# GpSimd's long operations in four pieces, and the first low weight part made by VectorE

## The chip, the cores and the metric

The kernel runs on one core of a Trainium2 chip. A core has five engines that the program feeds with one queue each: TensorE (PE: matrix products and transpositions), VectorE (DVE), ScalarE (ACT), GpSimd (POOL) and SyncE (SP, which here issues most DMA transfers). Engines wait for each other by semaphores. The metric is the time of one execution in device microseconds; the time before is the median of three runs.

## What is computed

The inputs are float32: q, k, v of 4 batches x 8 heads x 576 tokens x 64, and the weights of three stages. Cut to what matters:

```python
# 1. causal attention and a linear memory, mixed by a gate per head
a = softmax(mask(q @ k.T / 8));  local = a @ v
phi = where(x > 0, x, exp(x) - 1) + 1
mem = (phi(q) @ M_prev) / (phi(q) @ z_prev + 1e-6)
x = sigmoid(beta) * mem + (1 - sigmoid(beta)) * local     # -> 2304 x 512
# 2. a mixture of 8 experts: each token goes to the expert of its largest logit
e = argmax(x @ w_gate);  y = gate_w * sigmoid(x @ w_output_gate)[e] * (relu(x @ w1[e]) @ w2[e])
# 3. a gated layer
out = (sigmoid(y @ m2_gate) * (y @ m2_val)) @ m2_out
```

## The kernel before

The three stages follow one another: attention with the routing to 320 or 340 us, the experts to about 659, the gated layer to the end. Precision is kept by splitting operands into a high and a low part (x rounded by ScalarE, then x minus that by VectorE or GpSimd).

The attention works on 16 pairs of heads, two pairs to a group `gi` (8 groups). For a pair TensorE transposes q and k, forms the scores of both heads in the two halves of its array (`scores`, L373), VectorE subtracts the mask and takes the row extremes (`masked`, L402), ScalarE exponentiates (L410), TensorE transposes the result (L455), either VectorE or ScalarE copies it (`copy`, L301 and L299), and TensorE multiplies it with v (L489). The reciprocals of the row sums are made by `recip`: a `scalar_tensor_tensor` (L420), a reciprocal (L421), a cast (L422) and a subtraction (L423), all of VectorE and 9 columns wide, from tiles in SBUF.

Beside this, for each group, phi(q) is made: ScalarE's `phi_exp` (L269), then four operations of GpSimd in `phi_sum` (n = 0 to 3: a maximum with 0, L274, a minimum with 1, L276, their sum, L278, the product with z, L280), VectorE's `phi_norm` (the sum `nm` of 64 columns each, L285 to L288) and GpSimd's `phi_scale` (L292). All of GpSimd's are 128 x 1152 (18 blocks of 64).

When the eight heads of a batch are finished, `Routing` computes logits, the largest logit and its place (`first`, L864 to L869: O), the gate's factors in four steps (`factor_a` L885 to L889 and a sum L875 or L878; `factor_b`, ScalarE's two exponentials L893 and L894; `factor_c` L901 to L903; `factor_d` L907), and x is stored to DRAM (`x_turn`, `x_keep`, `x_store`). With the last batch `slots` counts the tokens of each expert (L946, L953 and on to L1030: A), `row_sel` makes Bm (L997), a product of both (L1047) gives the tokens' places, and GpSimd gathers the first two tiles of tokens (L1063).

The first expert's weights, eight parts of 128 x 1024, are split at the end of the attention: the high parts `wh` by ScalarE (L1154), the low parts `wl` by VectorE or GpSimd (L1159).

The order of all this is made by `Plan`, which takes each step with a rank, a cost per engine and what it needs, and writes the instructions in the order of a greedy list; a step that names two engines goes to the one that the plan has free first. What an operation really takes, or that one engine holds up another, is not in the plan.

Of the kernel before, what the change touches and what calls it, by code (L numbers as in the profile page):

```python
# [9 lines left out]
F32 = mybir.dt.float32  # L10
# [3 lines left out]
ALU = mybir.AluOpType  # L14
# [4 lines left out]
P = 128  # L19
B, H, S, D = 4, 8, 576, 64  # L20
HG = 4
NP = B * H // 2
NQ = 9
NK = 5
# [5 lines left out]
NT = NTOK // P  # L30
# [25 lines left out]
class Plan:  # L56
# [15 lines left out]
    def add(self, name, rank, cost, fn, needs=(), takes=(), uses=()):  # L72

        assert name not in self.steps, name
        self.steps[name] = (rank, cost, fn, tuple(needs), tuple(takes))
        for t in (*takes, *uses):
            self.users.setdefault(t, []).append(name)
# [48 lines left out]
class Attention:  # L126
# [142 lines left out]
        self.nc.scalar.activation(self.G[gi, "e"], self.G[gi, "q"], AF.Exp)  # L269

    def phi_sum(self, gi, n):
        nc, q, ph, e = self.nc, self.G[gi, "q"], self.G[gi, "ph"], self.G[gi, "e"]
        if n == 0:
            nc.gpsimd.tensor_scalar(ph, q, 0.0, None, ALU.max)  # L274
        elif n == 1:
            nc.gpsimd.tensor_scalar(e, e, 1.0, None, ALU.min)  # L276
        elif n == 2:
            nc.gpsimd.tensor_tensor(ph, ph, e, ALU.add)  # L278
        else:
            nc.gpsimd.tensor_tensor(e, ph, self.G[gi, "z"], ALU.mult)  # L280

    def phi_norm(self, gi):
        nc = self.nc
# [5 lines left out]

    def phi_scale(self, gi):  # L290
        pv = self.G[gi, "ph"].rearrange("p (a d) -> p a d", d=64)
        self.nc.gpsimd.tensor_tensor(pv, pv, self.G[gi, "nm"][:, :, None].to_broadcast([P, 18, 64]), ALU.mult)  # L292


    GROUPS = ((0, 1, 2), (3, 4))
# [212 lines left out]
    def run(self, ex, change):  # L508
# [8 lines left out]
        add = p.add  # L517
# [10 lines left out]
        for gi in range(NP * 2 // HG):  # L528
            u0 = gi * NQ * (HG // 2)
            r = u0 - 18  # L530
            for l in range(2):
                for i, nm in enumerate("qk"):
                    add(("L", nm, gi, l), r + 2 * l + i, {"SP": 1.6}, lambda e, a=(gi, nm, l): self.load_nat(*a),
                        needs=[("L", nm, gi, 0)] * l, takes=[] if l else [(nm + "n", gi)], uses=[(nm + "n", gi)] * l)
# [7 lines left out]
            for n, c in enumerate((3.06, 3.06, 2.57, 2.57)):  # L542
                needs = [("L", "q", gi, 1)] if n == 0 else [("phe", gi)] if n == 1 else [("phs", gi, n - 1), ("phs", gi, 0)]
# [7 lines left out]
        for pi in range(NP):  # L551
            gi, u0 = pi // 2, pi * NQ
            before = [("S", pi - 2, c) for c in ORDER] if pi > 1 else []
            for g in range(2):
                n = (384, 192)[g]
                r = u0 - 13 + g
                for nm in "qk":
                    kz = nm == "k" and g == 0
                    add(("X", nm, pi, g), r, {"PE": PO + n / 1200}, lambda e, a=(nm, pi, g): self.turn(*a),
                        needs=[("L", nm, gi, pi % 2)] + (before if nm == "q" else [("X", "k", pi, 0)] if g else []),  # L560
# [3 lines left out]
                    needs=[("X", "q", pi, g)] + [("qh", pi, 0)] * g, takes=[] if g else [("qT", pi)], uses=[("T", ("q", pi, g))] + [("qT", pi)] * g)  # L564
                add(("ql", pi, g), r, {"DV": dv(nq)}, lambda e, a=(pi, g, 1): self.q_part(*a),
                    needs=[("qh", pi, g)], uses=[("T", ("q", pi, g)), ("qT", pi)])
                if g:
# [3 lines left out]
                    needs=[("X", "k", pi, g)] + ([("kh", pi, 0)] if g else []), uses=[("T", ("k", pi, g)), ("kz", pi)])  # L571
# [4 lines left out]
                    needs=[("ph", gi)] + ([("X", "ph", pi, 0)] if g else []),  # L576
                    takes=[("T", ("ph", pi, g))] + ([] if g else [("phT", pi)]), uses=[("ph", gi)])
                add(("pp", pi, g), r, {"AC": ac(n), "DV": dv(n)}, lambda e, a=(pi, g): self.p_part(e, *a),
                    needs=[("X", "ph", pi, g)] + ([("pp", pi, 0)] if g else []),
# [81 lines left out]
        wide = [n for n in p.steps if n[0] in ("phn", "qh", "ql", "zh", "zl", "S", "m", "r", "rt", "rk", "b", "bc", "t", "v", "o", "os")]  # L661
        for n in range(8):
            add(("wh", n), 900 + n, {"AC": 0.95}, lambda e: ex.split_hi(),
                needs=[("w", 7), ("lc", B - 1, 1), *wide] + ([("wh", n - 1)] if n else []) + [("xc", NT - 1 if n else NT - 4)])
            late = [] if n < 1 else [("r4", B - 1)] if n < 2 else ["places"] if n < 5 else ["x1"]
            add(("wl", n), 900 + n, {"DV": 1.14} if n in (2, 3, 4, 5) else {"PL": 2.3},
                lambda e, n=n: ex.split_lo(n, self.nc.vector if e == "DV" else self.nc.gpsimd), needs=[("wh", n)] + late)
        for n in range(2):
            add(("f", n), 998, {"SP": 1.0}, lambda e: ex.load_part(), needs=[("wl", n)] + ([("f", n - 1)] if n else []))
        add("ahead", 999, {"SP": 3.0}, lambda e: ex.load_ahead(self.gather), needs=["x1"] + [("wl", n) for n in range(4)])  # L670
# [398 lines left out]
class Experts:  # L1069
# [84 lines left out]
        self.nc.scalar.activation(hi, t, AF.Copy)  # L1154
        self.half[n] = t, hi, lo, slot

    def split_lo(self, n, eng):
        t, hi, lo, slot = self.half.pop(n)
        eng.tensor_tensor(lo, t, hi.bitcast(F32), ALU.subtract)  # L1159
        if slot is not None:  # L1160
            self.free.append(slot)

# [579 lines left out]
```

## Time and profile before

| | |
|---|---|
| median of three runs | 1142.98 us (1142.48 to 1143.62) |
| the profiled execution | 1142.84 us, its span 1140.9 us |
| TensorE busy over the span | 1039.0 us (91%) |
| VectorE busy | 547.2 us (48%) |
| ScalarE busy | 457.2 us (40%) |
| GpSimd busy | 275.0 us (24%) |
| mean granted TensorE clock | 0.952 |

The profile is of one execution. "Busy" counts from an instruction's start to its end; an instruction that is held by something other than a semaphore counts as busy while it is held. "Granted clock" is the share of TensorE's full clock in a stretch: 1.00 is 2.4 GHz, 0.50 is 1.2 GHz. In the timeline an idle time in brackets stands before an instruction and names what ended it.

### The profile page before, as it was taken

The page shows a single profiled execution, that of the slowest core. Times are in us where ns is not written, and L with a number is a line of the kernel's source. Part 1 is how long each engine was busy: PE and PEld are TensorE (multiplying, and loading weights), DVE is VectorE, ACT ScalarE, POOL GpSimd, SP SyncE. Part 2 cuts the span into 40 slices and gives each one's busy share as a digit, 9 for nine tenths or more (in the row PEclk, how much of TensorE's full clock was granted, in tenths as well). Part 3 has the DMA queues.
Part 4 walks back from the last instruction along what each step waited for, and adds up shares of the span by engine and source line. Part 5 has one row for each costly group of instructions (what it writes and reads, how often), then busy time and mean ns, then how long its engine had stood idle before and what let it go on. Part 6 is the DMA issues. An engine that isn't in the chain of part 4 may idle for free. (4 is left out here: it accounts for less than half of the span.)

```text
span 1140.9 us, 16928 instructions
## 1 busy us (share of the span) xinstructions
PE 1039.0 (91%) x6181; PEld 886.2 (78%) x6181; DVE 547.2 (48%) x1266; ACT 457.2 (40%) x1049; POOL 275.0 (24%) x268
## 2 busy tenths in 40 slices
PE   6799798899959969988996969999999999999997
PEld 4566566566648959977995758999899999999996
DVE  6878778777566244225323869961212112121112
ACT  5676576566445244125313445531221212221211
POOL 8464443142057135016303500000110000100101
PEclk9799899889979989998998979999999999999999
DMA  6847324223049348116513556510010000100000
GB/s 121 137 88 169 94 66 104 50 60 98 1 141 322 114 128 274 38 46 217 168 39 98 167 160 195 184 55 1 29 56 1 28 28 1 56 1 1 28 1 28
DMA packets 111900, 102.52 MB, mean 90 GB/s; under 512 B 69520, under 2 KB 86928, under 8 KB 111760
## 3 DMA queue, kind: packets, MB, share of 16 engines
q1 hardware_dynamic: 107888, 88.18, 27.3%
q0 software_dynamic: 3872, 12.62, 3.4%
q8 instruction: 70, 1.15, 0.5%
q14 instruction: 70, 0.57, 0.2%
HBM read 84.49 MB, written 16.28 MB: 88 GB/s over the span
## 5 line engine op out<-in xcount | busy, mean ns | idle before, releaser
L1539 DVE TENSOR_TENSOR G<-G,pT 128x384 f32<-128x384 f32 (+1 forms) x74 | 40.1, 543 | 248.9 <-PE pT L1525 247.4
L1571 POOL DMA_INDIRECT out_dram<-o,rows x18 | 17.5, 971 | 463.8 <-ACT o L1567 213.2
L1546 ACT ACTIVATE Gh<-G 128x384 fp32r<-128x384 f32 (+1 forms) x74 | 38.2, 516 | 162.1 <-DVE G L1539 162.1
L410 ACT ACTIVATE Sm<-Sm,mx 128x512 f32<-128x512 f32 (+3 forms) x144 | 83.2, 579 | 31.0 <-DVE mx L402 30.6
L1535 ACT ACTIVATE G<-pH 128x384 f32<-128x384 f32 x72 | 35.4, 491 | 128.1 <-PE pH L1525 128.0
L1159 POOL TENSOR_TENSOR W<-raw,W 128x1024 fp32r<-128x1024 f32 x23 | 61.4, 2668 | 102.4 <-ACT W L1154 102.3
L402 DVE CUSTOM_DVE_ANT_0 Sm<-Sp,mask 128x512 f32<-128x512 f32 (+3 forms) x144 | 65.1, 482 | 25.1 <-PE T L455 13.1
L455 PE MATMUL T<-ident,Sm 128*128 128x128 f32 (+1 forms) x400 | 66.1, 304 | 11.1 <-DVE xt L301 6.0
L1556 PE MATMUL pX<-W,Gh 128*128 128x512 f32 x220 | 68.8, 394 | 0.0
L1154 ACT ACTIVATE W<-raw 128x1024 fp32r<-128x1024 f32 x60 | 61.7, 1054 | 16.7 <-DMA y_dram<-y 7.9
L455 PEld LDWEIGHTS T<-ident,Sm 128*128 128x128 f32 (+1 forms) x400 | 47.7, 151 | 24.1 <-DVE xt L301 6.2
L299 ACT ACTIVATE pt<-T 128x512 f32<-128x512 f32 (+4 forms) x128 | 49.9, 434 | 32.3 <-PE T L455 31.2
L489 PE MATMUL O<-pt,vn 128*64 128x192 f32 (+4 forms) x512 | 60.6, 357 | 0.0
L1544 DVE TENSOR_TENSOR Gl<-G,Gh 128x384 fp32r<-128x384 f32 (+1 forms) x74 | 40.4, 546 | 33.9 <-ACT Gh L1546 33.9
L1159 DVE TENSOR_TENSOR W<-raw,W 128x1024 fp32r<-128x1024 f32 x37 | 52.8, 1438 | 7.5 <-ACT W L1154 7.5
L1290 PE MATMUL pH<-W,xh 128*128 128x512 f32 x80 | 28.6, 503 | 28.7 <-issue 18.9
L373 PE MATMUL Sp<-kz,qT 64*128 64x512 f32 (+3 forms) x384 | 52.0, 382 | 2.0 <-DVE kz L346 1.3
L1525 PE MATMUL pT<-xh,W 128*128 128x384 f32 x264 | 52.8, 343 | 0.0
L1525 PE MATMUL pT<-yh,W 128*128 128x384 f32 x264 | 51.3, 336 | 0.0
L489 PEld LDWEIGHTS O<-pt,vn 128*64 128x64 f32 (+1 forms) x512 | 31.0, 139 | 23.1 <-issue 16.2
L1525 PE MATMUL pH<-yh,W 128*128 128x384 f32 x240 | 46.9, 337 | 1.4 <-DVE xl L1514 1.4
L1525 PEld LDWEIGHTS pT<-xh,W 128*128 128x128 f32 x264 | 47.4, 192 | 0.7
(331 smaller groups left out, 2468.3 us busy)
## 6 DMA issues: line engine op xcount, KB each, us to landing
raw<-in_moe_w_dram SPq DMA_DIRECT2D x60, 512.0 KB, 4.9
raw<-in_moe_w_gate_dram SPq DMA_DIRECT2D x12, 512.0 KB, 4.2
raw<-in_moe_w_val_dram SPq DMA_DIRECT2D x12, 512.0 KB, 3.6
raw<-in_moe_w_out_dram SPq DMA_DIRECT2D x12, 512.0 KB, 3.4
y_dram<-y SPq DMA_DIRECT2D x9, 513.0 KB, 3.2
qn<-in_q_dram SPq DMA_DIRECT2D x32, 128.0 KB, 3.0
kn<-in_k_dram SPq DMA_DIRECT2D x32, 128.0 KB, 2.7
zf<-in_z_prev_dram SPq DMA_DIRECT2D x32, 128.0 KB, 6.1
```

The lines of the kernel that those rows point to most:

```text
L299: self.nc.scalar.activation(out, in_, AF.Copy)
L373: nc.tensor.matmul(Sp[:, j, 0:n], lhsT=q[r, a, c * 128 : (c + 1) * 128], rhs=kz[r, k, 0:n], start=(p_ == 0), stop=(p_ == 2), skip_group_ch ...
L402: self.nc.vector.tensor_tensor_reduce(out=self.Sm[pi, n][:, k0:k1], in0=self.Sp[pi, c][:, j if n < 8 else si, 0 : k1 - k0], in1=mask, scal ...
L410: self.nc.scalar.activation(self.Sm[pi, n], self.Sm[pi, n], AF.Exp, scale=-1.0, bias=self.mx[pi, n][:, si : si + 1], accum_out=self.sums[p ...
L455: nc.tensor.transpose(T[:kr, o * 128 : (o + 1) * 128], self.Sm[pi, n][:, i * 128 : i * 128 + kr], self.ident)
L489: nc.tensor.matmul(O[j * 64 : (j + 1) * 64, q0 - q0b : q1 - q0b], lhsT=self.G[gi, "v"][:kr, i, 2 * l + j, :], rhs=PT[:kr, j, i, q0:q1], st ...
L1154: self.nc.scalar.activation(hi, t, AF.Copy)
L1159: eng.tensor_tensor(lo, t, hi.bitcast(F32), ALU.subtract)
L1525: nc.tensor.matmul(t, lhsT=w[:, k * P : (k + 1) * P], rhs=x[:, k, :], start=(m == k == 0), stop=(m == 2 and k == 3),)
L1539: nc.vector.tensor_tensor(t, t, p, ALU.mult)
L1544: nc.vector.tensor_tensor(l, t, hi.bitcast(F32), ALU.subtract)
L1556: nc.tensor.matmul(po[g][jj], lhsT=a[:, ts], rhs=w, start=(f == 0 and m == 0), stop=(f == NF - 1 and m == 2), skip_group_check=True,)
```

## The change

Each of GpSimd's five 128 x 1152 operations of a group is written as four instructions over the blocks 0 to 5, 5 to 10, 10 to 14 and 14 to 18, that is 320, 320, 256 and 256 columns. The first low part of the first expert's weights (`wl` 0) may be made by VectorE alone, the second (`wl` 1) by GpSimd in four pieces of 256 columns; the first high part no longer has to wait for the last logits. The costs in the plan stay.

```diff
--- before.py
+++ after.py
@@ -19,6 +19,7 @@
 P = 128
 B, H, S, D = 4, 8, 576, 64
 HG = 4
+PIECES = ((0, 5), (5, 10), (10, 14), (14, 18))
 NP = B * H // 2
 NQ = 9
 NK = 5
@@ -269,15 +270,17 @@
         self.nc.scalar.activation(self.G[gi, "e"], self.G[gi, "q"], AF.Exp)
 
     def phi_sum(self, gi, n):
-        nc, q, ph, e = self.nc, self.G[gi, "q"], self.G[gi, "ph"], self.G[gi, "e"]
-        if n == 0:
-            nc.gpsimd.tensor_scalar(ph, q, 0.0, None, ALU.max)
-        elif n == 1:
-            nc.gpsimd.tensor_scalar(e, e, 1.0, None, ALU.min)
-        elif n == 2:
-            nc.gpsimd.tensor_tensor(ph, ph, e, ALU.add)
-        else:
-            nc.gpsimd.tensor_tensor(e, ph, self.G[gi, "z"], ALU.mult)
+        nc = self.nc
+        for a, b in PIECES:
+            q, ph, e = (self.G[gi, nm][:, a * 64 : b * 64] for nm in ("q", "ph", "e"))
+            if n == 0:
+                nc.gpsimd.tensor_scalar(ph, q, 0.0, None, ALU.max)
+            elif n == 1:
+                nc.gpsimd.tensor_scalar(e, e, 1.0, None, ALU.min)
+            elif n == 2:
+                nc.gpsimd.tensor_tensor(ph, ph, e, ALU.add)
+            else:
+                nc.gpsimd.tensor_tensor(e, ph, self.G[gi, "z"][:, a * 64 : b * 64], ALU.mult)
 
     def phi_norm(self, gi):
         nc = self.nc
@@ -289,7 +292,9 @@
 
     def phi_scale(self, gi):
         pv = self.G[gi, "ph"].rearrange("p (a d) -> p a d", d=64)
-        self.nc.gpsimd.tensor_tensor(pv, pv, self.G[gi, "nm"][:, :, None].to_broadcast([P, 18, 64]), ALU.mult)
+        for a, b in PIECES:
+            nm = self.G[gi, "nm"][:, a:b, None].to_broadcast([P, b - a, 64])
+            self.nc.gpsimd.tensor_tensor(pv[:, a:b], pv[:, a:b], nm, ALU.mult)
 
 
     GROUPS = ((0, 1, 2), (3, 4))
@@ -661,10 +666,10 @@
         wide = [n for n in p.steps if n[0] in ("phn", "qh", "ql", "zh", "zl", "S", "m", "r", "rt", "rk", "b", "bc", "t", "v", "o", "os")]
         for n in range(8):
             add(("wh", n), 900 + n, {"AC": 0.95}, lambda e: ex.split_hi(),
-                needs=[("w", 7), ("lc", B - 1, 1), *wide] + ([("wh", n - 1)] if n else []) + [("xc", NT - 1 if n else NT - 4)])
+                needs=[("w", 7), *wide] + [("lc", B - 1, 1)] * (n > 0) + ([("wh", n - 1)] if n else []) + [("xc", NT - 1 if n else NT - 4)])
             late = [] if n < 1 else [("r4", B - 1)] if n < 2 else ["places"] if n < 5 else ["x1"]
-            add(("wl", n), 900 + n, {"DV": 1.14} if n in (2, 3, 4, 5) else {"PL": 2.3},
-                lambda e, n=n: ex.split_lo(n, self.nc.vector if e == "DV" else self.nc.gpsimd), needs=[("wh", n)] + late)
+            add(("wl", n), 900 + n, {"DV": 1.14} if n in (0, 2, 3, 4, 5) else {"PL": 2.3},
+                lambda e, n=n: ex.split_lo(n, *((self.nc.vector, 1) if e == "DV" else (self.nc.gpsimd, 4 if n < 2 else 1))), needs=[("wh", n)] + late)
         for n in range(2):
             add(("f", n), 998, {"SP": 1.0}, lambda e: ex.load_part(), needs=[("wl", n)] + ([("f", n - 1)] if n else []))
         add("ahead", 999, {"SP": 3.0}, lambda e: ex.load_ahead(self.gather), needs=["x1"] + [("wl", n) for n in range(4)])
@@ -1154,9 +1159,11 @@
         self.nc.scalar.activation(hi, t, AF.Copy)
         self.half[n] = t, hi, lo, slot
 
-    def split_lo(self, n, eng):
+    def split_lo(self, n, eng, parts=1):
         t, hi, lo, slot = self.half.pop(n)
-        eng.tensor_tensor(lo, t, hi.bitcast(F32), ALU.subtract)
+        w = 1024 // parts
+        for o in range(0, 1024, w):
+            eng.tensor_tensor(lo[:, o : o + w], t[:, o : o + w], hi.bitcast(F32)[:, o : o + w], ALU.subtract)
         if slot is not None:
             self.free.append(slot)
 
```

GpSimd, one group's phi (the last one): qn is q, e the exponential, zf is z, nm the factor, MB the memory matrix that is cleared. Before:

```order
L274 TENSOR_SCALAR ph<-qn 128x1152
L276 TENSOR_SCALAR e<-e 128x1152
L278 TENSOR_TENSOR ph<-ph,e 128x1152
L280 TENSOR_TENSOR e<-ph,zf 128x1152
L292 TENSOR_TENSOR ph<-ph,nm 128x1152
L245 MEMSET MB 128x256
```

After:

```order
L277 TENSOR_SCALAR ph<-qn 128x320 x2
L277 TENSOR_SCALAR ph<-qn 128x256 x2
L279 TENSOR_SCALAR e<-e 128x320 x2
L279 TENSOR_SCALAR e<-e 128x256 x2
L281 TENSOR_TENSOR ph<-ph,e 128x320 x2
L281 TENSOR_TENSOR ph<-ph,e 128x256 x2
L283 TENSOR_TENSOR e<-ph,zf 128x320 x2
L283 TENSOR_TENSOR e<-ph,zf 128x256 x2
L297 TENSOR_TENSOR ph<-ph,nm 128x320 x2
L297 TENSOR_TENSOR ph<-ph,nm 128x256 x2
L246 MEMSET MB 128x256
```

The order of the operations is the same, each in four pieces.

GpSimd, from the last Bm of the first three batches to the two gathers at the end of the attention (W is the split weight, raw its loaded float32, xn the gathered tokens). Before:

```order
L997 TENSOR_SCALAR Bm<-col,rf_3602,tok 128x128 x5
L1159 TENSOR_TENSOR W_4042<-raw_70,W_4042 128x1024
L878 TENSOR_TENSOR r_d<-r_d 128x5x4
L878 TENSOR_TENSOR r_d<-r_d 128x5x2
L878 TENSOR_TENSOR r_d<-r_d 128x5
L901 TENSOR_SCALAR r_d<-r_d 128x5
L902 TENSOR_SCALAR sid<-r_a 128x5
L903 TENSOR_TENSOR sid<-sid,r_d 128x5
L1159 TENSOR_TENSOR W_4042<-raw_71,W_4042 128x1024
L1063 DMA xn_80<-x_dram,kept 128x514
L1063 DMA xn_4046<-x_dram,kept 128x514
```

After:

```order
L883 TENSOR_TENSOR r_sel<-r_sel 128x5
L883 TENSOR_TENSOR r_d<-r_d 128x5x4
L883 TENSOR_TENSOR r_d<-r_d 128x5x2
L883 TENSOR_TENSOR r_d<-r_d 128x5
L906 TENSOR_SCALAR r_d<-r_d 128x5
L907 TENSOR_SCALAR sid<-r_sel 128x5
L908 TENSOR_TENSOR sid<-sid,r_d 128x5
L1002 TENSOR_SCALAR Bm<-col,rf_4264,tok 128x128
L1166 TENSOR_TENSOR W_4162<-raw_71,W_4162 128x256 x4
L1068 DMA xn_80<-x_dram,kept 128x514
L1068 DMA xn_4166<-x_dram,kept 128x514
```

The first low part has left GpSimd; ahead of the rows shown stand the four others of the last batch's `factor_a`, which VectorE made before. One Bm of the last batch has come in, and the second low part stands behind it in pieces.

VectorE, the last batch's routing, from the largest logits to the running counts `inc`. Before:

```order
L864 TENSOR_REDUCE r_mx<-L 128x5
L865 TENSOR_TENSOR r_t<-L,r_mx 128x40
L866 TENSOR_TENSOR r_t<-r_t,desc 128x40
L867 TENSOR_REDUCE r_vm<-r_t 128x5
L869 TENSOR_TENSOR O<-r_t,r_vm 128x5x8
L885 TENSOR_TENSOR r_d<-L,r_mx 128x40
L889 TENSOR_TENSOR r_sel<-O,L 128x40
L875 TENSOR_REDUCE r_a<-r_sel 128x5
L953 SCALAR_TENSOR_TENSOR inc_4122<-seg_502,T 128x144
```

After:

```order
L869 TENSOR_REDUCE r_mx<-L 128x5
L870 TENSOR_TENSOR r_t<-L,r_mx 128x40
L871 TENSOR_TENSOR r_t<-r_t,desc 128x40
L872 TENSOR_REDUCE r_vm<-r_t 128x5
L874 TENSOR_TENSOR O<-r_t,r_vm 128x5x8
L1166 TENSOR_TENSOR W_4162<-raw_70,W_4162 128x1024
L958 SCALAR_TENSOR_TENSOR inc_4244<-seg_508,T 128x144
```

The three of `factor_a` have left, and the first low part stands in their place. Further on VectorE makes four Bm instead of five, ahead of the reciprocal of the factors (L912, before L907) and not behind it. ScalarE makes the two exponentials of `factor_b` after two more high parts. The rows of TensorE and of SyncE are the same in both.

## Rows read from the trace of the kernel before

**Rows 1.** Busy table, 16 to 320 us: PE, PEld, DVE, ACT, POOL, clock, DMA share.

```profile
16.00:320.00 304.00, 273.55 (x1978) 190.70 (x1977) 223.58 (x685) 195.10 (x595) 118.78 (x65) 0.92 0.40 90
```

**Rows 2.** TensorE's waits, 20 to 320 us: us in total, times, longest.

```profile
PE Sp L380 <- DVE mx L402: 7.5, 1, 7.5
...
PE T L311 <- DVE xT L505: 6.1, 3, 2.2
...
PE T L455 <- DVE xt L301: 6.0, 1, 6.0
...
PE T L311 <- DVE pt L301: 3.8, 1, 3.8
```

**Rows 3.** Timeline, 39 to 55 us: start, duration, engine, line, operation, [idle before].

```profile
39.18 3.13 POOL L274 TENSOR_SCALAR ph<-qn 128x1152 f32<-128x1152 f32 x1
...
39.32 2.78 DVE L420 SCALAR_TENSOR_TENSOR rs<-sums,iog 128x9 f32<-128x9 f32 x1
...
42.28 3.12 POOL L276 TENSOR_SCALAR e<-e 128x1152 f32<-128x1152 f32 x1
...
42.38 3.05 DVE L422 CAST rc<-rs 128x9 fp32r<-128x9 f32 x1
...
46.03 0.48 PE L311 MATMUL T<-ident,ph 128*128 128x128 f32 x1 [3.80 <-DVE pt L301]
...
54.69 0.16 DVE L420 SCALAR_TENSOR_TENSOR rs<-sums,iog 128x9 f32<-128x9 f32 x1
```

**Rows 4.** VectorE's groups, 16 to 320 us: busy us, mean ns, idle before.

```profile
L420 DVE SCALAR_TENSOR_TENSOR rs<-sums,iog 128x9 f32<-128x9 f32 x16 | 11.7, 732 | 0.0
...
L422 DVE CAST rc<-rs 128x9 fp32r<-128x9 f32 x16 | 10.7, 668 | 0.6
...
L869 DVE TENSOR_TENSOR O<-r_t,r_vm 128x32 fp32r<-128x32 f32 (+1 forms) x3 | 5.5, 1828 | 0.1
...
L903 DVE TENSOR_TENSOR sid<-sid,r_a 128x4 f32<-128x4 f32 (+1 forms) x2 | 5.2, 2575 | 0.1
...
L423 DVE TENSOR_TENSOR rc<-rs,rc 128x9 f32<-128x9 f32 x16 | 5.0, 312 | 0.5
...
L901 DVE TENSOR_SCALAR r_a<-r_a 128x4 f32<-128x4 f32 (+1 forms) x2 | 2.8, 1397 | 0.1
```

**Rows 5.** Busy table, as rows 1, four half-clock stretches: first, last, their sum.

```profile
44.48:54.72 10.24, 8.69 (x34) 6.13 (x35) 6.54 (x21) 4.08 (x13) 6.21 (x3) 0.50 0.80 172
...
249.28:256.10 6.83, 6.26 (x30) 4.90 (x30) 4.45 (x19) 4.76 (x16) 0.00 (x0) 0.50 0.00 0
...
sum 23.89, PE 21.78 PEld 16.52 DVE 15.64 ACT 14.25 POOL 6.21; mean PE 5.45 PEld 4.13 DVE 3.91 ACT 3.56 POOL 1.55
```

**Rows 6.** Timeline of TensorE: nine transpositions at full and at half clock.

```profile
63.26 1.43 PE L455 MATMUL T<-ident,Sm 128*128 128x128 f32 x9 [0.47 <-ACT pt L299]
...
175.16 2.18 PE L455 MATMUL T<-ident,Sm 128*128 128x128 f32 x9
```

**Rows 7.** Timeline, 317 to 337 us: the end of the attention.

```profile
318.15 2.24 DVE L866 TENSOR_TENSOR r_t<-r_t,desc 128x40 f32<-128x40 f32 x1
...
323.26 2.33 DVE L972 CAST ranki<-rank 128x18 int32<-128x18 f32 x1
...
327.05 2.09 PE L1047 MATMUL T<-Bm,A 128*28 128x128 f32 x18 [5.61 <-DVE sid L907]
...
330.99 2.36 DVE L1159 TENSOR_TENSOR W<-raw,W 128x1024 fp32r<-128x1024 f32 x2
```

**Rows 8.** Timeline of GpSimd and VectorE, at 75 and 274 us.

```profile
75.47 2.65 POOL L280 TENSOR_TENSOR e<-ph,zf 128x1152 f32<-128x1152 f32 x1
...
79.64 1.34 DVE L285 TENSOR_REDUCE nm<-e 128x18 f32<-128x1152 f32 x1
...
273.88 0.79 POOL L878 TENSOR_TENSOR r_d<-r_d 128x16 f32<-128x16 f32 x3 [6.53 <-ACT r_d L893]
```

**Rows 9.** GpSimd's groups, 16 to 320 us: the five Bm.

```profile
L997 POOL TENSOR_SCALAR Bm<-col,rf,tok 128x128 fp32r<-128x128 f32 x5 | 4.2, 841 | 0.3 <-DVE rf L982 0.3
```

## The prediction

> **What bounds the kernel now.** I read the busy table by stretch first. From 16 to 320 us, the loop of the attention stage, TensorE works 273.55 of 304.00 us at a mean granted clock of 0.92 [rows 1]. So TensorE is the bound there, and about 30 us of it are holes. The list of TensorE's waits says who ends them: VectorE, in four places or kinds, 7.5 us before a score product, 6.1 us in three waits before a transposition of k, 6.0 us and 3.8 us [rows 2]. That is 23.4 us.
>
> The timeline shows what VectorE does in such a hole [rows 3]. At 39.32 a division of 9 columns takes 2.78 us; the same instruction takes 0.16 us at 54.69. It ends at 42.10, and GpSimd's 1152-column operation, which began at 39.18, ends at 42.31. GpSimd's next one begins at 42.28; the cast at 42.38 takes 3.05 us and ends with that one. TensorE then starts again at 46.03 after 3.80 us. So some of VectorE's instructions are held until GpSimd's running operation is over, and they get in between two GpSimd operations even where the second follows at once.
>
> The groups of VectorE's instructions give the whole amount [rows 4]. Less 0.16 us (0.2 for the routing ones) for each, the held time is 11.7 - 2.6 = 9.1 us on L420, 10.7 - 2.7 = 8.0 on L422, 5.0 - 2.6 = 2.4 on L423, 5.5 - 0.6 = 4.9 on L869, 5.2 - 0.4 = 4.8 on L903 and 2.8 - 0.4 = 2.4 on L901: 31.6 us. By the timeline these fall in six places: B at 39, C at 89, E at 166, G at 244 (two long holds each, in the four instructions of `recip`), and D at 115 and F at 193 (four each, in the routing of a finished batch): 16 holds. The Trainium skill, "SBUF — State Buffer", Who interferes with whom, says that such a VectorE instruction (two inputs in SBUF, or a two-port mode) and a GpSimd one shut each other out for the whole instruction, and that the one issued second waits. The trace agrees, 2.78 us against 0.16.
>
> **Pieces of the long operations.** Each of the 40 operations of eight groups becomes four instructions of 320, 320, 256 and 256 columns: 120 more on GpSimd, the order of TensorE and SyncE unchanged, that of VectorE and ScalarE unchanged until the last batch is routed. A hold now lasts at most a piece: 3.12 x 320/1152 = 0.87 us for the one-input form [rows 3], 2.65 x 320/1152 = 0.74 for the two-input one [rows 8]. A first hold is met at a random point; a second comes some 0.3 us after the first got in, since a short instruction lies between. I take 0.5 us each. The bounds are none at all, and a whole piece of 0.8.
>
> - B: held 2.78 + 3.05 - 0.33 = 5.5 us before, 1.0 after. The 4.5 us saved exceed the hole: 3.8 us gone.
> - C, E, G: the rest of the `recip` holds is 19.5 - 5.5 = 14.0 us, some of it outside; about 4 each, 1.0 after. The holes are 6.1 us in all, 2 each, and the saving is larger: 6.1 gone.
> - D, F: four holds each, (4.9 + 4.8 + 2.4)/2 = 6.1 or more per place, 2.0 after. Their holes of 7.5 and 6.0 us shrink by 4.5 each: 9.0 gone.
>
> Together **18.9 us**; with 0.8 us a hold D and F give 2.9 each and C, E and G perhaps 5 in all, so 14.6; with no hold left all 23.4.
>
> **The clock.** After each of these holes the granted clock stood at 0.50, the 1.2 GHz level: from 44.48 to 54.72 at B, and so on to 249.28 to 256.10 at G [rows 5]. In the four stretches of B, C, E and G TensorE was busy 21.78 of 23.89 us. Elsewhere in the loop, away from holes, the clock was at 1.00. Nine transpositions took 2.18 us in the stretch after E and 1.43 at 63.26 at full clock [rows 6]: 0.75 of 2.18, 34%. If the hole goes, I expect the half-clock stretch behind it to go too, since no other cause stands near it: 0.34 x 21.78 = **7.4 us**. The bounds are 0 (the clock falls all the same) and half of 21.78, 10.9. D and F keep a hole of 1.5 to 3 us, so I leave their half-clock stretches as they are.
>
> **The end of the attention.** The first low part W (`wl` 0) goes from GpSimd to VectorE. On GpSimd it held VectorE in the routing of the last batch: 2.24 us on L866 at 318.15, where 0.2 would do, so 2.0. The second low part held the cast L972 for 2.33 us at 323.26, so 2.1 [rows 7]. In the new order the steps `r_d`, `r_sel` and the sum (`factor_a`) go to GpSimd in that place, VectorE does the low part itself right after O, 2.36/2 = 1.2 us [rows 7], and GpSimd does the second low part in four pieces after the last Bm. VectorE's low part lies in the chain O, counts, slots, but it fills the 0.6 us in which VectorE did `factor_a` and waited for the counts: net 0.6. One Bm of five goes to GpSimd, 0.84 us [rows 9], behind `factor_c`, which waits for an exponential that ScalarE now makes after two more high parts; I reckon that it ends with VectorE's last Bm or up to 0.7 us later. So 2.0 + 2.1 - 0.6 - 0.4 = **3.1 us** sooner for the product with Bm, which stood at 327.05 after 5.61 us of waiting [rows 7], and for the gathers behind it. GpSimd's four pieces stand ahead of the gathers; they end before the row numbers are there by about what is gained. Bounds: 1 and 4.1.
>
> **What the pieces cost.** A piece has a fixed cost that no row shows by itself. Three small dependent ones take 0.79 us [rows 8], so at most 0.26 each with their columns; the lower bound is 0, where the next piece starts while the last one ends, as 42.28 stands before 42.31 [rows 3]. GpSimd is idle most of the loop, 118.78 of 304.00 us busy [rows 1], and VectorE comes to the sum `nm` long after it is ready, but for one group: its last operation ends at 75.47 + 2.65 = 78.12 and VectorE's reduction starts at 79.64 [rows 8]. Slack 1.5 us, less a sum of 15 extra pieces x 0.16 (nearer to the small ones) = 2.4: VectorE waits **0.9 us** there, bounds 0 and 15 x 0.26 - 1.5 = 2.4. [...]
>
> **Sum.** 18.9 + 7.4 + 3.1 - 0.9 = 28.5 us. The profiled execution took 1142.84 us, its span 1140.9, and 1142.84 - 28.5 = 1114.3; the median of the runs is 1142.98, 0.14 higher, so **1114.5 us**. After the attention nothing changes in any engine's order.
>
> **Rivals.**
> 1. The holes go, the clock doesn't come back: 1114.5 + 7.4 = 1122 us. For it: half-clock stretches stand behind holes of only 2 us, so it takes little. Against it: the loop is at 1.00 wherever TensorE had no hole.
> 2. A piece is dear. The one short one-input instruction in the trace, Bm of 128 columns, takes 0.84 us [rows 9], while 128 columns at 3.12/1152 are 0.35; that leaves 0.49 us fixed. Then `nm` is late by 15 x 0.49 - 1.5 = 5.9 us, perhaps in a second group too, and a hold grows to some 0.8 us: 14.6 + 3.7 + 3.1 - 5.9 to 11.8 = 9.6 to 15.5 saved, 1127 to 1133. Against it: Bm takes two per-partition operands, the pieces none.
> 3. Slower: GpSimd's queued pieces follow so closely that VectorE does not get in between pieces of one operation, only at its end. Then every hold stays and grows by three fixed costs, 3 x 0.26 = 0.8 us; 16 x 0.8 = 12.5 us, of which 23.4/31.6 reached TensorE: 9.3 us more, 3.1 less at the end, 1149 us. It decides from the first piece on, at B. Against it: VectorE got in at 42.10, when GpSimd's next operation was ready.
> 4. Another engine takes the holes over (ScalarE waits for VectorE's maxima in the same stretches): little gained, 1136 to 1142. Against it: ScalarE is busy 195.10 of 304 us [rows 1].
> 5. No hold is left and D's and F's clock comes back as well: 23.4 + 10.9 + 4.1 = 38 us, 1105.
>
> **How the numbers follow.** Forecast 0.50 (1109 to 1120), rival 1 0.17, rival 2 0.12, rival 3 0.07, rival 4 0.06, rival 5 0.08. A range from 1105 to 1131 leaves out rivals 3 and 4 and the edges of 2 and 5, some 0.18. A measurement of this kernel tells about 0.2% from no change, 2.3 us. Faster: all but rival 3 and half of rival 4, 0.90; the same 0.03; slower 0.07.
>
> **What would show it.** In the trace after: L420 and L422 at most 0.9 us each, their groups near 6 and 6 us; TensorE's waits for VectorE in the loop near 5 us; granted clock 1.00 at the places of C, E and G; the product with Bm about 28 us earlier than 327.05; VectorE's reduction `nm` waiting for GpSimd in one group at most. I am wrong if holds still end with the fourth piece, if the four pieces together take over 4 us, or if the loop gains and the experts start no sooner.

## The result and the profile after

The changed kernel takes **1106.45 us** (median of four runs, 1103.55 to 1110.49) against 1142.73 us before, a ratio of 0.9684 with a 95% interval of 0.9652 to 0.9717. The forecast was 1114.5 us, with a range of 1105 to 1131. The profiled execution of the changed kernel is the slowest of the four: 1110.49 us, span 1108.6. Lines after L274 have moved by 3 to 7: L420 to L423 are L425 to L428 now, and GpSimd's L274, L276, L278, L280 and L292 are L277, L279, L281, L283 and L297.

The busy table for the stretch of [rows 1]: TensorE (first number behind the comma) is busy for 277.94 of the 304 us in place of 273.55, though the stretch now reaches into the experts, and the granted clock (behind POOL) is 0.95 in place of 0.92.

```profile
16.00:320.00 304.00, 277.94 (x2048) 195.97 (x2047) 214.64 (x721) 205.83 (x609) 155.12 (x211) 0.95 0.44 105
```

TensorE's waits in that stretch (total, times, longest), which answer to [rows 2]. The 7.5, 6.1, 6.0 and 3.8 us for VectorE are gone; 2.0, 1.8 and 1.6 us are the largest of that kind in the loop.

```profile
PE T L1052 <- DVE A L1035: 3.5, 1, 3.5
...
PE T L460 <- ACT xt L304: 3.2, 2, 2.5
...
PE T L460 <- DVE xT L510: 2.0, 1, 2.0
PE Sp L385 <- DVE mx L407: 1.8, 1, 1.8
PE T L460 <- DVE kz L351: 1.6, 1, 1.6
```

VectorE's groups, as in [rows 4] (total, mean ns): the cast fell from 10.7 to 4.4 us, L869, L901 and L903 (now L874, L906 and L908) from 13.5 to 2.6, but L425 only from 11.7 to 8.4.

```profile
L425 DVE SCALAR_TENSOR_TENSOR rs<-sums,iog 128x9 f32<-128x9 f32 x16 | 8.4, 524 | 0.5 <-ACT Sm L415 0.5
...
L428 DVE TENSOR_TENSOR rc<-rs,rc 128x9 f32<-128x9 f32 x16 | 4.6, 289 | 0.6
L427 DVE CAST rc<-rs 128x9 fp32r<-128x9 f32 x16 | 4.4, 276 | 0.6
...
L874 DVE TENSOR_TENSOR O<-r_t,r_vm 128x32 fp32r<-128x32 f32 (+1 forms) x4 | 1.1, 274 | 0.1
...
L906 DVE TENSOR_SCALAR r_a<-r_a 128x4 f32<-128x4 f32 (+1 forms) x2 | 0.9, 448 | 0.1
...
L908 DVE TENSOR_TENSOR sid<-sid,r_a 128x4 f32<-128x4 f32 (+1 forms) x2 | 0.6, 296 | 0.1
```

Where the 8.4 us come from, the timeline of B shows (start, duration, engine; "x4" are four pieces). The division starts at 50.23 and ends at 54.08. Six pieces end in between, two of L281's and all four of L283's; VectorE is passed over at five of these ends and gets in behind the last. TensorE waits 2.05 us behind it.

```profile
47.99 3.06 POOL L281 TENSOR_TENSOR ph<-ph,e 128x320 f32<-128x320 f32 x4
...
50.23 3.85 DVE L425 SCALAR_TENSOR_TENSOR rs<-sums,iog 128x9 f32<-128x9 f32 x1
...
51.01 3.05 POOL L283 TENSOR_TENSOR e<-ph,zf 128x320 f32<-128x320 f32 x4
...
54.12 0.21 DVE L426 RECIPROCAL rs<-rs 128x9 f32<-128x9 f32 x1
...
55.26 0.66 PE L460 MATMUL T<-ident,Sm 128*128 128x128 f32 x4 [2.05 <-DVE xT L510]
```

For the account I cut the time at three points that both kernels pass with the same work done: the start of the last division of `recip` (301.6 us before, 276.3 after), the product with Bm (327.05, 298.22) and the issue of the load of the token rows for the last stage (671.27, 638.16). Before:

```profile
16.00:301.60 285.60, 255.49 (x1835) 179.30 (x1835) 216.32 (x667) 188.32 (x581) 116.73 (x64) 0.92 0.42 93
301.60:327.05 25.45, 18.48 (x146) 11.72 (x146) 14.06 (x41) 12.98 (x23) 6.20 (x8) 0.95 0.22 73
327.05:671.27 344.22, 303.62 (x1775) 265.67 (x1776) 148.60 (x217) 127.70 (x206) 122.26 (x129) 0.93 0.45 147
```

After:

```profile
16.00:276.30 260.30, 244.72 (x1837) 172.13 (x1836) 193.73 (x667) 187.95 (x581) 134.37 (x184) 0.98 0.45 102
276.30:298.22 21.92, 18.42 (x146) 11.69 (x146) 10.54 (x38) 10.29 (x21) 3.06 (x8) 0.96 0.24 76
298.22:638.16 339.94, 301.21 (x1759) 263.04 (x1760) 151.67 (x215) 128.88 (x207) 122.03 (x138) 0.93 0.45 149
```

In the loop the same TensorE work takes 255.49 - 244.72 = 10.8 us less (the clock: 0.98 granted in place of 0.92), and its idle time falls from 30.1 to 15.6, 14.5 us less. The end of the attention is 3.5 us shorter. The experts are 4.3 us shorter too, where I had expected nothing.

### The profile page after: what moved, and what is told of

Read it like the earlier page. It is cut to its first block, busy times and chain, and to the rows that moved or that the text cites. A ratio compares the mean times of both kernels' runs of the same rounds, so it can differ in the third digit from the quotient of the medians.

```text
span 1108.6 us, 17069 instructions
## 1 busy us (share of the span) xinstructions
PE 1028.2 (93%) x6181; PEld 878.6 (79%) x6181; DVE 525.0 (47%) x1263; ACT 456.2 (41%) x1049; POOL 289.1 (26%) x396
## 3 DMA queue, kind: packets, MB, share of 16 engines
q8 instruction: 68, 1.11, 0.4%
## 5 line engine op out<-in xcount | busy, mean ns | idle before, releaser
L1542 ACT ACTIVATE G<-pH 128x384 f32<-128x384 f32 x72 | 35.4, 491 | 132.4 <-PE pH L1532 132.3
L1166 POOL TENSOR_TENSOR W<-raw,W 128x1024 fp32r<-128x1024 f32 (+1 forms) x25 | 56.7, 2274 | 66.8 <-ACT W L1159 66.8
L460 PE MATMUL T<-ident,Sm 128*128 128x128 f32 (+1 forms) x400 | 61.2, 287 | 8.9 <-ACT xt L304 3.2
L460 PEld LDWEIGHTS T<-ident,Sm 128*128 128x128 f32 (+1 forms) x400 | 44.3, 142 | 21.0 <-ACT xt L304 4.0
L1166 DVE TENSOR_TENSOR W<-raw,W 128x1024 fp32r<-128x1024 f32 x38 | 56.9, 1508 | 6.8 <-ACT W L1159 6.8
L378 PE MATMUL Sp<-kz,qT 64*128 64x512 f32 (+3 forms) x384 | 49.0, 361 | 1.9 <-DVE kz L351 0.8
L1532 PEld LDWEIGHTS pT<-xh,W 128*128 128x128 f32 x264 | 47.4, 192 | 3.0 <-DVE G L1546 2.2
L1297 PE MATMUL pH<-W,xh 128*128 128x512 f32 x80 | 26.4, 472 | 24.8 <-issue 24.3
```

The costliest lines, as they stand in the source:

```text
L378: nc.tensor.matmul(Sp[:, j, 0:n], lhsT=q[r, a, c * 128 : (c + 1) * 128], rhs=kz[r, k, 0:n], start=(p_ == 0), stop=(p_ == 2), skip_group_ch ...
L460: nc.tensor.transpose(T[:kr, o * 128 : (o + 1) * 128], self.Sm[pi, n][:, i * 128 : i * 128 + kr], self.ident)
L1166: eng.tensor_tensor(lo[:, o : o + w], t[:, o : o + w], hi.bitcast(F32)[:, o : o + w], ALU.subtract)
L1532: nc.tensor.matmul(t, lhsT=w[:, k * P : (k + 1) * P], rhs=x[:, k, :], start=(m == k == 0), stop=(m == 2 and k == 3),)
```

## The experiments

Each kernel is described by its difference to the changed kernel, unless it says otherwise. "Held" is the sum, from 14 to 292 us, of what VectorE's instructions took beyond the shortest of their kind in any of these kernels, where that is over 0.15 us. "Experts" is the time from the product with Bm to the load of the token rows. Those two columns and the product are of the profiled execution, the median is of all runs; all times are in us.

| kernel | held | product with Bm | experts | median |
|---|---|---|---|---|
| before | 32.7 | 327.1 | 344.2 | 1142.7 |
| changed | 10.5 | 298.2 | 339.9 | 1106.5 |
| changed, again | 7.2 | 291.7 | 337.8 | 1103.2 |
| phi_only | 10.1 | 303.3 | 335.2 | 1109.5 |
| end_only | 32.6 | 322.9 | 345.6 | 1140.4 |
| end_shift | 19.0 | 301.9 | 345.2 | 1119.4 |
| one_in | 12.0 | 293.7 | 345.8 | 1110.8 |
| one_in_8 | 11.9 | 295.2 | 336.8 | 1104.9 |
| two_in | 19.2 | 305.8 | 337.3 | 1113.7 |
| nine | 9.6 | 306.2 | 335.8 | 1121.8 |
| nine_break, one run | 4.3 | 324.7 | 341.2 | 1136.7 |
| reduce1 | 13.3 | 305.5 | 343.9 | 1122.0 |
| reduce4 | 1.2 | 292.4 | 335.5 | 1098.9 |

### The two parts apart: phi_only and end_only

phi_only is the kernel before with the pieces of phi; end_only is the changed kernel with

```diff
-PIECES = ((0, 5), (5, 10), (10, 14), (14, 18))
+PIECES = ((0, 18),)
```

> Only the pieces of the five long operations of phi; the low weight parts stay as in the kernel before. The theory of the sum: the loop's gain (25.3 us at the last reciprocal, 301.6 before, 276.3 in the changed kernel) comes from the pieces alone, and the end of the attention gains nothing: product with Bm near 301, 1114 to 1118 us. Rival, that what was gained behind the attention (about 5 us in the profiled execution, more by the medians) is the clock's and not the end's: 1109 to 1112 us.

> Only the new low weight parts; phi's operations in one piece each. The theory of the sum: about 3 us (product with Bm near 324), 1139 to 1141 us, and the holds in the loop as before. Rival, that the new end is what brings the extra gain behind the attention too: product near 324 but 1134 to 1137 us.

Measured: 1109.48 us (0.9697, 0.9667 to 0.9727) and 1140.40 us (0.9975, 0.9958 to 0.9991). end_only did what the sum said: the stretch up to the product is 21.84 us in place of 25.45, the holds in the loop are as before, and the experts are no shorter (345.6). phi_only has the loop's gain and experts of 335.2 us. So the unforeseen gain comes with the pieces, not with the new end; whether through the clock, as my rival had it, was open.

### The loop without phi: no_phi

```diff
-        self.nc.scalar.activation(self.G[gi, "e"], self.G[gi, "q"], AF.Exp)
+        self.nc.scalar.activation(self.G[gi, "ph"], self.G[gi, "q"], AF.Exp)
...
     def phi_sum(self, gi, n):
+        pass
...
     def phi_scale(self, gi):
+        pass
```

> GpSimd's five operations of phi are left out (phi is the exponential alone and is not divided by its sum), so the experts get other tokens and only the time up to the first gathers can be compared. If the holds by GpSimd are what is left of VectorE's holes: no hold of the four instructions of the reciprocal, the half-clock stretch at 40 to 47 us gone, the last reciprocal near 270 us against 276.3 (3.7 us of the longest hold and the clock behind it). Rival, that the holes left are the loop's own: 275 to 277 us.

Measured: no hold above 0.2 us on any of the four instructions, and the last division at 269.8 us, as expected. One expectation failed: the half-clock stretch at 37 to 44 us is there without any hold, so it isn't the hold's. Ahead of it TensorE waits 1.58 us for `kz` (35.0 to 36.6), as it waits 1.57 us for it in the kernel before and in the changed one. The row is TensorE's work in the stretch, 6.94 of 7.00 us at a granted clock of 0.51:

```profile
37.00:44.00 7.00, 6.94 (x33) 4.81 (x31) 4.51 (x21) 5.06 (x16) 0.00 (x0) 0.51 0.71 79
```

### More pieces: nine, and nine_break

```diff
-PIECES = ((0, 5), (5, 10), (10, 14), (14, 18))
+PIECES = tuple((i, i + 2) for i in range(0, 18, 2))
```

> Nine pieces of 128 columns in place of four. A piece costs about 0.15 us more than its columns, so a group of five operations takes 25 x 0.15 = 3.8 us longer on GpSimd, and VectorE's sum waits for it: 1106 to 1113 us; a single hold lasts at most 0.5 us if VectorE gets in at each end of a piece. Rival, that it can be shut out over many ends of pieces (as at 50.23 us in the changed kernel, 3.85 us over five of them): single holds of 1 us and more again, several of them.

Measured: 1121.76 us (1114.72 to 1127.16; 0.9829, 0.9792 to 0.9865), slower than the changed kernel. The rival is right about the holds: there are single ones of 3.79 us at 74.47, 3.61 at 192.25 and 0.98 at 124.79. VectorE's sum `nm` waits for GpSimd besides, 4.1 us in two groups, as expected; how the loss divides between the two I did not separate. In the first of the holds VectorE waits out all nine pieces of 0.46 us:

```profile
74.46 3.77 POOL L283 TENSOR_TENSOR e<-ph,zf 128x128 f32<-128x128 f32 x9
74.47 3.79 DVE L425 SCALAR_TENSOR_TENSOR rs<-sums,iog 128x9 f32<-128x9 f32 x1
```

So a row of pieces can act like one long operation, and the end of a piece is a chance to get in, not a right. nine_break is nine with a short GpSimd instruction behind each piece of the sum and of the product; the sum's is shown:

```diff
                 nc.gpsimd.tensor_tensor(ph, ph, e, ALU.add)
+                nc.gpsimd.tensor_scalar(self.tiny[:, 1:2], self.tiny[:, 0:1], 1.0, None, ALU.min)
...
```

> Nine pieces, and after each piece of the sum and of the product a GpSimd instruction of one tensor operand and one column. Theory, that VectorE is shut out over a row of pieces when two-operand pieces follow each other without a break: no hold over 1 us. Rival, that a break of another short GpSimd instruction does not let it in: holds of 2 to 4 us as with nine pieces (3.79 and 3.61 there). GpSimd gets longer, so the time is 1118 us or more.

Measured: 1136.7 us, one run. The longest hold is 1.28 us, over two pieces and two short instructions; the next is 0.84. My bound of 1 us did not hold, yet holds of 3 us did not come either. The time says nothing about the holds: VectorE's sum `nm` waits 19.1 us for the longer GpSimd work, in all eight groups. One profile of a thing that varies between executions does not settle it.

### The changed kernel once more: again

> The changed kernel once more, for a second profile of it. If the hold of 3.85 us at 50.23 comes from the order of the instructions, it stands there again within 0.5 us; if it is a matter of chance, it is gone or elsewhere. 1103 to 1111 us.

Measured: 1103.23 us (1100.11 to 1113.28). In its profile (1102.36 us) the hold at 50 us is gone, the longest is 0.74 us over the shortest, and L425 takes 4.5 us in place of 8.4. The last division stands at 269.8 us, 6.5 us earlier than in the first profile of the same program.

```profile
L425 DVE SCALAR_TENSOR_TENSOR rs<-sums,iog 128x9 f32<-128x9 f32 x16 | 4.5, 281 | 0.5 <-ACT Sm L415 0.5
```

So the long hold isn't fixed by the order of instructions; it comes in some executions. What decides it stays open. phi_only had one of 4.16 us at the same place. That goes with the spread of the runs, 1100 to 1113 us for this program against 1138 to 1146 for the one before, but the executions that weren't profiled can't be explained one by one.

### VectorE's instructions in another form: reduce4 and reduce1

The sums lie beside a copy of the gate in one tile (16 short ScalarE copies more), and three of the four instructions become reductions; the 1e-9 under the division is left out, and reduce1 has phi in one piece besides.

```diff
-        nc.vector.scalar_tensor_tensor(t, self.sums[pi], 1e-9, self.iog[:, hp], ALU.add, ALU.mult)
+        nc.vector.tensor_reduce(t, self.both[pi].rearrange("p a c -> p c a"), AX.X, ALU.mult)
         nc.vector.reciprocal(t, t)
-        nc.vector.tensor_copy(rc.bitcast(F32R)[:, 0:NQ], t)
-        nc.vector.tensor_tensor(rc[:, NQ:], t, rc[:, 0:NQ], ALU.subtract)
+        with nc.allow_low_precision(reason="a reduction over one element"):
+            nc.vector.tensor_reduce(rc.bitcast(F32R)[:, NQ : 2 * NQ], rc[:, 0:NQ].rearrange("p (c a) -> p c a", a=1), AX.X, ALU.add)
+        nc.vector.tensor_reduce(rc[:, 2 * NQ :], rc[:, 0 : 2 * NQ].rearrange("p (a c) -> p c a", a=2), AX.X, ALU.subtract)
...
```

> The changed kernel, with the four instructions of the reciprocal written so that three of them are reductions over one or two elements (a product over sum and gate, a sum over one element, a difference over two) and none has two operands. Theory, that what is left of the holds falls on these instructions for their operands' sake: no hold of 0.2 us or more on them, and none of 3.7 us over six pieces as at 50.23; last reciprocal near 271 to 273 us, 1100 to 1105 us. Rival, that VectorE's short instructions are held whatever their form: holds as in the changed kernel, 1104 to 1110 us.

> The same reductions, but phi's five operations in one piece each as before. Theory, that the holds and no other effect of the pieces make the gain: B, C, E and G have no hold (20.5 us of held time gone), D and F keep theirs (4 each); last reciprocal near 284 us, 1115 to 1123 us. Rival, that the pieces do something else for the loop: 1130 us or more.

Measured: reduce4 1098.90 us (0.9608, 0.9569 to 0.9646), the best of all (its interval lies below the changed kernel's first one, 0.9652 to 0.9717, and overlaps with that of again, 0.9616 to 0.9733); reduce1 1121.98 us (0.981, 0.9779 to 0.9842). None of the three reductions was held, with or without pieces; in reduce4 they take 163 to 174 ns in the mean:

```profile
L431 DVE TENSOR_REDUCE rc<-rc 128x9 f32<-128x18 f32 x16 | 2.8, 174 | 0.5
L427 DVE TENSOR_REDUCE rc<-sums 128x9 f32<-128x18 f32 x16 | 2.7, 166 | 0.3 <-ACT Sm L417 0.3
L430 DVE TENSOR_REDUCE rc<-rc 128x9 fp32r<-128x9 f32 x16 | 2.6, 163 | 0.5
```

The last reciprocal stands at 270.8 us in reduce4 and 283.8 in reduce1 (271 to 273 and 284 expected). So it is the holds themselves that cost the loop its time, not some other effect that the pieces take away: reduce1 cuts none of phi's operations and gains 22 us (1144.01 us for the kernel before beside it), of which the new end is worth 2.3 by end_only. The Trainium skill, "SBUF — State Buffer", Who interferes with whom, says that a reduction never contends with GpSimd on this chip, while an instruction with two inputs in SBUF and a copy or cast in a two-port mode can; these rows agree.

In reduce1 the routing at D and F still has its holds (13.3 us), TensorE still waits 7.47 us at 114.27 and 5.95 at 188.47, and half-clock stretches still stand there, 10.2 us from 108 and 6.8 from 187. In the changed kernel the hole at F is gone and that at D is down to 1.8 us (the wait for mx above), and D and F are at full clock. In again and reduce4 the hole at D has the same 1.8 us, and 3.4 us behind it are at a granted clock of 0.50. So the long half-clock stretches of D and F go with the long holes, but a hole of 1.8 us is followed by half clock in one execution and not in another.

### Which operations matter: one_in and two_in

one_in cuts only the maximum and the minimum (one tensor operand), two_in only the other three. one_in's edit, in `phi_sum` and in `phi_scale`; two_in has `n > 1` in the first and leaves the second:

```diff
-        for a, b in PIECES:
+        for a, b in PIECES if n < 2 else ((0, 18),):
...
-        for a, b in PIECES:
+        for a, b in ((0, 18),):
```

> Four pieces for the maximum and the minimum alone (one tensor operand); the sum, the product and the scaling in one piece. The holds at B, the first of C and two of four at D and F go (about 13 us of held time), those of 2.4 us behind the two-operand forms stay (C, E, G, and one each at D and F). By the terms of the sum: 3.8 + about 9 us of holes, 3 to 7 of clock, 3 of the end: 1120 to 1127 us. Rival, that the two-operand forms carry the gain: 1130 to 1136 us.

> The other half: four pieces for the sum, the product and the scaling, one for the maximum and the minimum. Holds at C, E and G shrink to some 0.5 us each, those at B, D and F stay but for one each. By the terms of the sum: 6 us of holes, 4 of clock, 3 of the end and 1 to 4 at D and F: 1126 to 1131 us. The two halves together should give about the whole, 36 us less the 3 of the end counted twice.

Measured: 1110.82 us (0.9718, 0.9682 to 0.9754) and 1113.68 us (0.9748, 0.9712 to 0.9784), both far better than expected. I had added the two halves up, and they do not add. Up to the product with Bm one_in alone gains 33.3 us, as much as the whole change (28.8 and 35.4 in its two profiles); two_in gains 21.2 there, and another 6.9 in the experts, which have another cause (next section). one_in shows why. At E it still has one hold of 2.45 us, and from 140 to 170 us the list of TensorE's waits is empty.

```profile
150.89 2.45 DVE L427 CAST rc<-rs 128x9 fp32r<-128x9 f32 x1
```

Before, E had two such holds and a hole of 2 us. At B and G one_in has one hold each as well, 2.38 and 2.43 us, and TensorE waits 0.6 us at most. TensorE's queue thus covers about one hold of 2.4 us at these places; the second is what costs. It is not so everywhere: at 26.83 us one hold of 2.16 us is followed by a wait of 1.4 us. One half of the pieces takes away one of the two.

### The experts' 9 us: end_shift and one_in_8

By the table the experts take 344 to 346 us in five kernels and 335 to 341 in the others. end_shift tests the count of GpSimd's instructions, on end_only:

```diff
+        for _ in range(5 * (n < 3)):
+            nc.gpsimd.memset(self.tiny, 0.0)
```

> The kernel with only the new low weight parts, and in the loop 15 tiny GpSimd instructions more for each group (one column set to zero): 120 in all, as many as the pieces add, with no operation cut. Theory, that the time gained behind the attention (345 us from the product with Bm to the rows' load without the two-operand pieces, 335 to 340 with them) hangs on how many GpSimd instructions the program has: 335 to 340 us there and 1131 to 1136 us in all. Rival, that it hangs on when the experts start or on the pieces themselves: 345 us there, 1139 to 1142 us.

Measured: the experts took 345.2 us, so the count of GpSimd's instructions is not it. The time, 1119.35 us (0.9798), was outside both forecasts: I had not reckoned with the loop. The short instructions ahead of whole operations brought the held time from 32.6 to 19.0 us, mostly one hold a place in place of two, and the product came 21 us sooner than in end_only. Nothing was cut there.

What does go with the short experts: up to the product with Bm, TensorE's queue holds 88 waiting instructions in the kernels with long experts and 96 in the others, by a count of the trace's records. The eight come with phi's scaling in pieces, one for each group, at the transposition of phi. They put all code behind them eight instructions further on. one_in_8 adds eight TensorE instructions to one_in in another way:

```diff
+        for _ in range(2 if pi in (3, 6, 9, 12) else 1):
             self.nc.tensor.transpose(T[0 : 2 * NQ, 0:P], self.rc[pi], self.ident)
```

> The kernel with four pieces for the maximum and the minimum alone, and four of its 16 transpositions of the reciprocals made twice (the same result written again): eight TensorE instructions more ahead of the experts, 0.2 us of work each at most. In the traces the stage behind the attention takes 344 to 346 us where TensorE's queue holds 88 waiting instructions up to the product with Bm, and 335 to 341 where it holds 96. Theory, that these eight move TensorE's code against the blocks in which it is loaded, and that the experts' branches then wait less for code: 335 to 341 us there, and 1100 to 1105 us against 1110.8 without them. Rival, that the eight waits go with something else in the phi pieces that shortens the stage: 344 to 346 us there, 1109 to 1114 us.

Measured: experts 336.8 us against 345.8, and 1104.85 us (1102.60 to 1113.41; 0.9698, 0.9644 to 0.9752) against 1110.82. The gain in the experts is of one profile each (two profiles of the changed kernel differ by 2.1 us there), and the intervals of the whole times overlap. TensorE's waits in the second half of the experts show where. one_in first, then one_in_8:

```profile
PE pH L1297 <- issue: 17.2, 2, 11.5
PE pH L1514 <- issue: 6.4, 1, 6.4
PE pX L1514 <- DMA yn<-y_dram: 4.1, 1, 4.1
```

```profile
PE pH L1298 <- issue: 11.6, 2, 9.1
...
PE pH L1515 <- PEq L1413: 3.7, 1, 3.7
...
PE pX L1515 <- DMA yn<-y_dram: 0.9, 1, 0.9
```

"issue" is time in which TensorE waits for no semaphore that the profile shows. It stands where one expert's code branches to the next one's (L1297, L1298) and where the last stage begins (L1514, L1515). The kernel before has 15.9, 6.7 and 4.1 us in these rows, the changed kernel 12.0, 3.7 and 0.4. The page of a profile counts transfers of instructions: on the queue q8 70 of 1.15 MB in all before, 68 of 1.11 MB after, 16 KB each. It is 70 in all five kernels of the table with long experts and 68 in all the others. Before, then after:

```profile
q8 instruction: 70, 1.15, 0.5%
```

```profile
q8 instruction: 68, 1.11, 0.4%
```

The Trainium skill, "Runtime: NRT & Kernel Launch", Instruction fetch mechanics, says that code comes in blocks of 16 KiB, 256 instructions, and that a taken branch to a block that is not there stalls the engine until it is fetched. The 16 KB transfers and the waits at the branches agree. So a shift of the code by eight instructions goes with 9 us less in the experts and 6 us less in the medians of one_in_8 and one_in; for the change it is luck, not merit. That the code's place in the blocks is the cause is argued from the count of transfers and from where the waits stand: which block each branch misses I did not trace.

## Why the prediction was right, and where it was not

- **Holds at the end of a piece.** The mechanism was right: the routing's holes at D and F and those at C, E and G went with the holds, but for 1.8 us at D, of which 1.4 stand in no_phi without any hold. No_phi and reduce4 show that hardly anything else holds these instructions (0.2 us at most in no_phi). The holes gave 14.5 us in this profile and, by the same cuts, (285.60 - 255.49) - (253.80 - 243.06) = 19.4 in the profile of again; the term was 18.9. TensorE's waits for VectorE in the loop came to 9.9 us, and to 5.9 in again; near 5 were forecast. The assumption behind it, that a hold lasts at most a piece, failed in one place: at B, 3.85 us over six pieces, as above, ending with the fourth piece of L283, which I had named as a sign of being wrong. That is the mechanism of rival 3, which I had for every hold or none; it happens in some.
- **The clock.** Mis-sized: 7.4 expected, 10.8 and 12.4 us measured. I left the half-clock stretches of D and F as they were because a hole of 1.5 to 3 us would stay. At D 1.8 us did stay, but the clock did not fall behind it in this profile; that step, that a hole of this size keeps its half-clock stretch, was wrong here. In turn B gave back less than all: half clock stood there from 37.6 to 41.1 and 44.5 to 54.7 us before, and from 40.6 to 47.4 after, ahead of the long hold. The windows at B, C and D show 0.79, 1.00 and 1.00 (the third number from the end):

```profile
39.00:55.00 16.00, 13.88 (x86) 9.48 (x84) 12.60 (x35) 8.75 (x27) 15.05 (x20) 0.79 0.64 132
86.00:91.00 5.00, 5.00 (x40) 3.54 (x37) 4.21 (x18) 3.56 (x12) 5.00 (x7) 1.00 0.88 229
106.00:121.00 15.00, 12.00 (x90) 8.49 (x86) 9.21 (x39) 10.13 (x31) 13.22 (x16) 1.00 0.72 178
```

- **The end of the attention.** 3.1 us expected, 25.45 - 21.92 = 3.5 measured; end_only alone gives the same 3.6 there and 2.3 in the medians.
- **What the pieces cost.** Four pieces of the product, L283, take 3.05 us (at 51.01 above) where one took 2.65 [rows 8], 0.13 for each extra piece; 0.16 was reckoned. The 0.9 us that VectorE should wait for the sum `nm` did not come: in the loop VectorE has no wait for GpSimd at that line. Rival 2's 0.49 us for a piece was wrong. With nine pieces that wait did come, 4.1 us.
- **"After the attention nothing changes in any engine's order."** True of the order, and the step that failed for the time: 4.3 us in this profile, 6.4 in again, most likely from where the code lies. I read no row of the experts for this, though the 15.9 us of "issue" were in the trace.

In this profile the terms come to 14.5 + 10.8 + 3.5 = 28.8 us where 28.5 were forecast. That the sums agree is luck: the holes gave 4.4 us less than their term, and the clock 3.4 more, the end 0.4 more and the pieces' 0.9 us of cost did not come. The experts' 4.3 us on top make 33.1 of the 33.1 us at the load of the rows; the profiled time fell by 1142.84 - 1110.49 = 32.4. The median lies 4 us lower than this execution. The again profile, with 35.4 us up to the product and 6.4 in the experts, shows what a run without the long hold looks like. The forecast's median missed the two gains, the code's and the rest of the clock's, and 1106.45 us lies near the lower end of its range; the median of again, 1103.23, lies below it.

## What to carry to other kernels

A short VectorE instruction that takes 3 us in place of 0.16, and ends with a GpSimd operation, may be held by it. Give it a form that isn't held where it has one (reductions were not, in 96 instructions of two kernels), and cut the other engine's work into pieces for the rest: the end of a piece lets the short instruction in often but not always, and nine pieces did worse than four. Here both together were best, 1098.9 us, against 1106.5 with the pieces and 1122.0 with the reductions alone, all three with the new end. Holds don't add up: look at how many fall in one place, because at three places TensorE's queue covered one of 2.4 us and not two. And when a kernel with branches gets faster in a part that wasn't changed, count the instructions ahead of the branches before crediting the change.

## What the runs showed of the hardware that I had not expected

- VectorE was passed over at up to five ends of pieces in a row (changed, phi_only) and up to eight (nine), always with the division L425; the cast and the subtraction, which follow within 0.5 us, were passed over at one end at most in these kernels. Between two executions of one program such a hold came and went. What decides it stays open.
- GpSimd instructions of one column set to zero, 0.1 us each, ahead of uncut operations, removed 14 of 33 us of held time (end_shift against end_only).
- With eight TensorE instructions more ahead of them the experts were 9 us shorter (one_in_8: 345.8 to 336.8), at waits behind branches (17.2 to 11.6 and 6.4 to 3.7 us in all).
